# Reordering the output products of a fused attention and gated-FFN kernel: raw operands first, two pairs over two PSUM banks

## The chip, the core and the metric

The kernel runs on one core of a Trainium2 chip. The metric is the time of one execution on the device in microseconds (us). Before the change it is 850.09 us, the median of three runs (850.04 to 850.29). One more run was taken with the hardware profiler on: its span is 847.7 us, and all line numbers and profile times below come from it. The mean granted TensorE clock was 0.992 of full speed.

## What is computed

Two stages follow each other, over 4 batches of 6016 tokens with 256 channels:

```
qn = q / (norm of q over the tokens + 1e-6);  kn likewise
s  = kn^T @ qn / tau                          # 256 x 256 for each batch
a  = softmax(s)
x  = v @ a                                    # 6016 x 256 for each batch
gate = sigmoid(x @ w_gate);  val = x @ w_val  # 256 -> 1536
out  = (gate * val) @ w_out                   # 1536 -> 256, float32
```

The kernel never forms x. It multiplies the small softmax matrix into w_gate and w_val once for each batch (the tiles gh_G and gh_H), and so goes from v straight to gate and val.

## The kernel before

**Chunks and slots.** Tokens are worked on in chunks of 4 tiles of 128 tokens: 12 chunks for each batch (NCH), the last of them with 3 tiles. In a chunk the loop over f runs over 12 blocks of 128 hidden channels (FC = 12); one step of f is called a slot here. In a slot `glu` (line 460) issues two matmuls into ps_gate and two into ps_val (512 tokens wide), ScalarE takes the sigmoid of ps_gate into g_sb (line 481), and VectorE multiplies ps_val by it and writes one block of hT in bf16 (line 482). ps_gate and ps_val have two PSUM banks each.

**Output products.** The last product, hT with w_out, is done one chunk later, spread over the slots of the next chunk. It uses a scheme with seven products instead of eight for a 2 x 2 block product, in which the two token tiles of a pair p and tile p + 2 are one dimension, the two halves of the hidden channels the contraction, and the two halves of the 256 output channels the third. Of the seven products (PRODUCTS, line 33), n = 0 and 1 read hT itself; n = 2 to 6 read sums of hT blocks, which VectorE makes with `a_sum` (line 488, A_SUMS). Each product is 6 accumulating matmuls of 128 columns, so a chunk of 4 tiles has 2 pairs x 7 x 6 = 84 of them, called products in the rest of this text and counted from 0. The sums of the first half of the hidden channels (g = 0) are made in the chunk itself in slots 6 to 10, those of the second half (g = 1) in slots 0 to 4 of the next chunk.

**Banks and evictions.** Products 0 to 3 of a pair (n below FIRST_BANK) fill one PSUM bank of the pool pso, which has two, and products 4 to 6 another. When a bank is complete, `evict` (line 559) is put on the list `pending`; `flush()` (line 601), called after `glu` in each slot, issues it: a ScalarE copy into m_sb (line 564), and after a pair's second bank `combine` (line 515), five GpSimd operations (lines 522 to 528) that add the seven products up to out_sb. The last chunk of a batch has 3 tiles: one pair, and one tile whose product is done plainly (`single`, 12 matmuls of 256 columns). `store()` (line 606) writes out_sb to memory from SyncE's queue.

**The next batch beside it.** `side_work` (line 702) spreads the preparation of the next batch over the slots of the present one: loads of q and k, the score matmuls (ps_s, two of 256 columns about every second slot), squares on ScalarE (line 231), their accumulation on VectorE (line 269), and towards the end of the batch the folds of the accumulators (`acc_fold`, lines 279 to 287, six steps in consecutive slots from slot 2 of chunk 8), the norms (slot 9 of chunk 9), their root, their inversion (`wide_inv`, lines 309 and 310), scaling (line 320), exponentials (line 378), and the new gh tiles in chunk 11.

**Blocks.** The root and the exponentials need another activation table than the sigmoid. So at the end of chunks 9 and 10 a block stands after slot 11: half of the chunk's products (42) are held back and run there while ScalarE loads tables and works. In batch 3 there is no next batch, and so none of this.

The order on each engine is the order of the program: the kernel is recorded under a manual schedule. `run_work` (line 592) takes products from the list so that the remaining ones are spread evenly over the remaining slots, 7 to a slot in an ordinary chunk.

Of the kernel before, what the change touches and what calls it, by code (L numbers as in the profile page):

```python
# [16 lines left out]
A_SUMS = (  # L17
    ((0, 1), ALU.subtract, (1, 1)),
    ((0, 0), ALU.add, (1, 1)),
    ((0, 0), ALU.add, (0, 1)),  # L20
    ((1, 0), ALU.add, (1, 1)),
    ((1, 0), ALU.subtract, (0, 0)),
)
# [16 lines left out]
    (4, 4),  # L40
)
FIRST_BANK = 4


@with_exitstack
def kernel(
# [26 lines left out]
    B, N, C = q.shape  # L73
# [4 lines left out]
    FC = DFF // P  # L78
# [4 lines left out]
    NCH = (NT + TPC - 1) // TPC  # L83
# [446 lines left out]
    def out_work(b, ci):  # L530

        nt = groups[ci][1]
        half = nt // 2
        hT = hts[b, ci]
        work = []

        def product(state, p, n, i):
            a, w = PRODUCTS[n]
            bank, first = (0, 0) if n < FIRST_BANK else (1, FIRST_BANK)
            if n == first and i == 0:  # L540
                state[bank] = pso.tile([P, CH], FP32, tag="o", name="ps_o")
            g, j = divmod(i, FC // 4)
            if isinstance(a, tuple):
                lhsT = hT[:, 2 * i + a[1], ds((a[0] * half + p) * P, P)]
            else:
                lhsT = sums[b, ci, g][:, a, j, ds(p * P, P)]
            rhs = w_out_sb[:, 2 * i + w[0], ds(w[1] * P, P)] if isinstance(w, tuple) else w_sums[:, w, i, :]
            mm(
                state[bank][:, ds((n - first) * P, P)],
                lhsT,  # L550
                rhs,
                start=(n == first and i == 0),
                stop=(i == FC // 2 - 1),
                skip_group_check=True,
            )
            if i == FC // 2 - 1 and n in (FIRST_BANK - 1, len(PRODUCTS) - 1):
                pending.append((evict, state, bank, p))

        def evict(state, bank, p):
            if bank == 0:  # L560
                state["m"] = mpool.tile([P, len(PRODUCTS), P], FP32, tag="m", name="m_sb")
            n0, n1 = (0, FIRST_BANK) if bank == 0 else (FIRST_BANK, len(PRODUCTS))
            m = state["m"]
            nc.scalar.copy(m[:, n0:n1, :], state[bank][:, : (n1 - n0) * P].rearrange("p (n c) -> p n c", c=P))  # L564
            if bank == 1:
                combine(b, ci, p, m)
                if p == half - 1 and nt % 2 == 0:
                    stores.append((b, ci))

        def single(state, s, f):  # L570
            if f == 0:
                state["ps"] = pso.tile([P, CH], FP32, tag="o", name="ps_o")
            mm(state["ps"][:, :C], hT[:, f, ds(s * P, P)], w_out_sb[:, f, :], f == 0, f == FC - 1)
            if f == FC - 1:
                pending.append((evict_single, state, s))

        def evict_single(state, s):
            nc.scalar.copy(out_tile(b, ci)[:, s, :], state["ps"][:, :C])
            stores.append((b, ci))

        for p in range(half):
            state = {}
            for n in range(len(PRODUCTS)):
                for i in range(FC // 2):
                    work.append((1, product, state, p, n, i))
        if nt % 2:
            state = {}
            for f in range(FC):
                work.append((2, single, state, nt - 1, f))
        return work  # L590

    def run_work(work, share, keep=0):

        upto = sum(w[0] for w in work[: len(work) - keep]) * share
        done = 0
        while len(work) > keep and done < upto:
            cost, fn, *args = work.pop(0)
            fn(*args)
            done += cost

    def flush():
        while pending:
            fn, *args = pending.pop(0)
            fn(*args)

# [96 lines left out]
    def side_work(b):  # L702


        side = {}

        def at(slot, fn, *a):
            side.setdefault(divmod(slot, FC), []).append((fn, a))

        for ci in range(NCH):  # L710
            nb, nci = (b, ci + 1) if ci + 1 < NCH else (b + 1, 0)
            lb, lci = (b, ci + 2) if ci + 2 < NCH else (b + 1, ci + 2 - NCH)
            if (nb, nci) == (0, 1):
                at(8, lambda: transpose_v(0, 1, psm.tile([P, TPC * CB, P], BF16, tag="m", name="ps_tp")))
            elif nb < B:
                at(ci * FC + 2, transpose_v, nb, nci)
            if lb < B:
                at(ci * FC + 0, load_v, lb, lci)
            if (b, ci) == (0, 0):
                for i in range(FC // TPC):  # L720
                    at(i, load_w_out, i)
                    at(i + 2, sum_w_out, i)
        n = b + 1
        if n == B:
            return side
        first, last = (14 if b == 0 else 0), 8 * FC
        for g, (t0, nt) in enumerate(groups):
            s0 = first + g * (last - first) // NCH
            if b == 0:
                at(max(0, s0 - 12), load_qk, n, t0, nt)  # L730
            elif s0 >= 24:
                at(s0 - 24, load_qk, n, t0, nt)
            for u in range(nt):
                at(first + (t0 + u) * (last - first) // NT, score, n, t0, u)
            if g == 0:
                at(s0, acc_start, n)
            for i, (fn, w) in enumerate(((acc_square, 0), (acc_add, 0), (acc_square, 1), (acc_add, 1))):
                at(s0 + 1 + 2 * i, fn, n, g, w)
        if n + 1 < B:
            for g, (t0, nt) in enumerate(groups[:3]):  # L740
                at(NCH * FC - 24 + 8 * g, load_qk, n + 1, t0, nt)
        for i in range(6):
            at(8 * FC + 2 + i, acc_fold, n, *divmod(i, 3))
        at(9 * FC + 9, norms_mm, n)
        table = nc.scalar.preload_act_table
        for ci, s, *call in (
            (9, 0, wide_sqrt, n),
            (9, 0, table, ACT.Sigmoid),
            (9, 1, wide_inv, n, 0),
            (9, 2, wide_inv, n, 1),  # L750
            (10, 0, table, ACT.Exp),
            (10, 0, wide_scale, n),
            (10, 0, exps, n, 0),
            (10, 0, exps, n, 1),
            (10, 0, table, ACT.Sigmoid),
        ):
            side.setdefault((ci, FC + s), []).append((call[0], call[1:]))
        at(11 * FC + 0, sums_both, n)
        at(11 * FC + 0, gh_tiles, n)
        for i in range(len(gh_order)):  # L760
            at(11 * FC + min(i + 1, FC - 1), gh, n, i, *((pss, "s"), (psm, "m"))[i % 2])
        return side
# [6 lines left out]
    for b in range(B):  # L769
        side = side_work(b)  # L770
        for ci in range(NCH):
            block = b + 1 < B and ci in (9, 10)
            early = 1 if block else 2 if (b, ci) == (B - 1, NCH - 1) else 0
            for f in range(FC):
                first = (b, ci, f) == (0, 0, 0)
                glu(b, ci, f, (lambda: gh(0, 4, pso, "o", act=False)) if first else None)
                flush()
                if prev is not None:
                    if f == 4:
                        store()  # L780
                    if f < len(A_SUMS):
                        a_sum(*prev, 1, f)
                    held = len(work) if not block or f == 0 else held
                    run_work(work, 1 / max(1, FC - early - f), held // 2 if block else 0)
                if f >= FC // 2 and f - FC // 2 < len(A_SUMS) and (b, ci) != (B - 1, NCH - 1):
                    a_sum(b, ci, 0, f - FC // 2)
                for fn, a in side.get((ci, f), ()):
                    fn(*a)
                if (b, ci) == (0, 0):
                    for i in gh_first.get(f, ()):  # L790
                        gh(0, i, pso, "o")
            if prev is not None and block:
                flush()
                for s in range(3):
                    for fn, a in side.get((ci, FC + s), ()):
                        fn(*a)  # L796
                    run_work(work, 1 / (2 - s) if s < 2 else 1)
                flush()
            prev = (b, ci)
            if prev != (B - 1, NCH - 1):  # L800
                work = out_work(*prev)
# [40 lines left out]
```

## Time and profile before

| | us |
|---|---|
| median of the timed runs | 850.09 |
| span of the profiled run | 847.7 |
| head, until the first slot | 41.2 |
| batch 0, chunks 0 to 11 | 207.1 |
| batch 1 | 204.1 |
| batch 2 | 203.8 |
| batch 3, without the last chunk | 167.4 |
| last chunk and end | 24.1 |

The stages are read from the timeline, from the first ps_gate matmul of a chunk to that of a later one. Within a batch the chunks have different limits: chunks 0 to 8 carry the score matmuls and the squares of the next batch, chunks 9 and 10 end in blocks, chunk 11 makes the gh tiles, and batch 3 has the output work alone.

### The profile page before, as it was taken

Reading aid. Unit: us, or ns where it says so; the run is one execution under the profiler, and the core shown is the slowest. Engines: PE = TensorE matmul, PEld = TensorE weight load, DVE = VectorE, ACT = ScalarE, POOL = GpSimd, SP = SyncE. Lnnn points to the kernel's source line nnn. Section 1 sums busy time; section 2 is a strip of 40 time slices with the busy share of each in tenths; the row PEclk is TensorE's granted clock in tenths of the full one; section 3 lists DMA queues with packets and bytes.
Section 4 is the critical chain, followed back from the end, with each engine's and each line's share of the span. In section 5 each row is a group of like instructions: output and inputs, shape, how many; then the busy total and the mean of one; then the engine's idle time right before and its main releaser. Section 6 shows DMA issues by size and latency. Waiting matters only on the chain.

```text
span 847.7 us, 17813 instructions
## 1 busy us (share of the span) xinstructions
PE 798.8 (94%) x6760; PEld 499.0 (59%) x6772; DVE 741.2 (87%) x1236; ACT 531.7 (63%) x900; POOL 424.7 (50%) x623
## 2 busy tenths in 40 slices
PE   3799999999899999999989999999999999999996
PEld 2446666655566666665556666665565566666665
DVE  5688999999888999899978999999997988898884
ACT  3666667656766666665666667666576555555553
POOL 3564655443553656454544464645334355455543
PEclk9799999999999999999999999999999999999999
DMA  9976676432549556422275666622332422322401
GB/s 220 215 138 110 102 122 109 96 67 52 100 81 158 82 99 124 86 62 51 65 129 100 94 118 106 121 51 57 78 61 51 93 52 50 88 63 53 92 27 69
DMA packets 77926, 78.23 MB, mean 92 GB/s; under 512 B 50704, under 2 KB 55824, under 8 KB 77840
## 3 DMA queue, kind: packets, MB, share of 16 engines
q0 software_dynamic: 21216, 38.02, 27.2%
q1 hardware_dynamic: 56336, 38.48, 20.1%
q8 instruction: 53, 0.87, 0.4%
q10 hardware_dynamic: 288, 0.59, 0.2%
q14 instruction: 33, 0.27, 0.1%
HBM read 78.64 MB, written 24.64 MB: 122 GB/s over the span
## 4 chain that ended last, share of the span: by engine, by line
PE 73%; DVE 8%; ACT 7%; DMA 6%; issue 4%; POOL 2%; POOLq 0%; ACTq 0%; DVEq 0%
PE ps_gate L119 24%; PE ps_val L119 23%; PE ps_o L119 21%; DMA k_sb<-in_k_dram 6%; DVE sums L499 4%; DVE hT L482 4%; PE ps_s L119 3%; ACT g_sb L481 2%; PE ps_gh L119 2%; ACT sq L231 2%; ACT m_sb L564 1%; ACT L796 1%; POOL out_sb L525 0%; POOL m_sb L523 0%; DVE acc L269 0%
## 5 line engine op out<-in xcount | busy, mean ns | idle before, releaser
L481 ACT ACTIVATE g_sb<-ps_gate 128x512 f32<-128x512 f32 (+1 forms) x576 | 338.6, 588 | 273.0 <-PE ps_gate L119 259.1
L482 DVE TENSOR_TENSOR hT<-ps_val,g_sb 128x512 bf16<-128x512 f32 (+1 forms) x576 | 387.7, 674 | 78.1 <-ACT g_sb L481 71.0
L119 PE MATMUL ps_val<-vT,gh_H 128*128 128x512 bf16 (+1 forms) x1152 | 337.5, 374 | 3.7 <-DVE hT L482 3.4
L119 PE MATMUL ps_gate<-vT,gh_G 128*128 128x512 bf16 (+1 forms) x1152 | 337.5, 375 | 0.5
L499 DVE TENSOR_TENSOR sums<-hT 128x768 bf16<-128x768 bf16 (+1 forms) x470 | 305.2, 649 | 0.0
L522 POOL TENSOR_TENSOR m_sb<-m_sb 128x256 f32<-128x256 f32 x91 | 65.9, 724 | 383.4 <-ACT m_sb L564 383.4
L119 PEld LDWEIGHTS <-sums 128*128 128x128 bf16 x2730 | 187.9, 98 | 109.0 <-DVE sums L499 21.2
L119 PEld LDWEIGHTS <-gh_H 128*128 128x128 bf16 x1152 | 112.7, 98 | 136.8 <-issue 8.0
L119 PE MATMUL ps_o<-w_sums,sums 128*128 128x128 bf16 x1638 | 154.4, 219 | 1.9 <-DVE sums L499 1.7
L119 PE MATMUL ps_o<-w_out_sb,sums 128*128 128x128 bf16 x1092 | 109.9, 219 | 11.6 <-DVE sums L499 11.4
L119 PEld LDWEIGHTS <-hT 128*128 128x128 bf16 x1176 | 83.4, 98 | 55.3 <-issue 9.8
L525 POOL TENSOR_TENSOR out_sb<-m_sb 128x128 f32<-128x128 f32 x182 | 114.8, 650 | 0.0
L119 PEld LDWEIGHTS <-gh_G 128*128 128x128 bf16 x1152 | 96.8, 98 | 14.5 <-DVE gh_G L431 0.4
L119 PE MATMUL ps_o<-w_sums,hT 128*128 128x128 bf16 x1092 | 91.6, 219 | 8.6 <-ACT m_sb L564 8.3
L564 ACT COPY m_sb<-ps_o 128x512 f32<-128x512 f32 (+1 forms) x182 | 95.4, 528 | 0.1
L119 PE MATMUL ps_s<-k_sb,q_sb 128*128 128x256 bf16 x376 | 71.8, 295 | 17.9 <-DMA k_sb<-in_k_dram 10.6
L523 POOL TENSOR_TENSOR m_sb<-m_sb 128x256 f32<-128x256 f32 x91 | 81.1, 891 | 7.1
L528 POOL TENSOR_TENSOR out_sb<-m_sb 128x256 f32<-128x256 f32 x91 | 77.7, 853 | 0.0
L231 ACT ACTIVATE sq<-k_sb 128x1024 bf16<-128x1024 bf16 (+2 forms) x44 | 44.8, 1026 | 15.0 <-DMA k_sb<-in_k_dram 14.8
L269 DVE TENSOR_TENSOR acc<-acc,sq 128x1024 bf16<-128x1024 bf16 (+1 forms) x66 | 50.6, 766 | 0.0
L119 PEld LDWEIGHTS <-q_sb 128*128 128x128 bf16 x376 | 33.7, 105 | 23.5 <-issue 11.9
L231 ACT ACTIVATE sq<-q_sb 128x1024 bf16<-128x1024 bf16 (+2 forms) x36 | 36.5, 1015 | 0.2 <-DVE acc L659 0.2
(78 smaller groups left out, 276.6 us busy)
## 6 DMA issues: line engine op xcount, KB each, us to landing
out_dram<-out_sb SPq DMA_DIRECT2D x44, 512.0 KB, 3.4
v_sb<-in_v_dram POOLq DMA_DIRECT2D x44, 256.0 KB, 5.3
q_sb<-in_q_dram POOLq DMA_DIRECT2D x35, 256.0 KB, 6.9
k_sb<-in_k_dram POOLq DMA_DIRECT2D x35, 256.0 KB, 7.8
q_sb<-in_q_dram POOLq DMA_DIRECT2D x4, 512.0 KB, 12.7
k_sb<-in_k_dram POOLq DMA_DIRECT2D x4, 512.0 KB, 15.1
w_f<-in_moe_w_out_dram SPq DMA_DIRECT2D x3, 512.0 KB, 15.5
out_dram<-out_sb SPq DMA_DIRECT2D x3, 384.0 KB, 6.4
```

The source lines that it names most:

```text
L119: nc.tensor.matmul(out, lhsT=lhsT, rhs=rhs, start=start, stop=stop, **kw)
L231: nc.scalar.activation(out=sq[:, :nt, :], in_=src[:, :nt, :], func=ACT.Square)
L269: nc.vector.tensor_tensor(out=acc[:, :nt, :], in0=acc[:, :nt, :], in1=st[b]["sq", w][:, :nt, :], op=ALU.add)
L481: nc.scalar.activation(out=g_sb[:, :n], in_=ps_gate[:, :n], func=ACT.Sigmoid)
L482: nc.vector.tensor_tensor(out=hts[b, ci][:, f, :n], in0=ps_val[:, :n], in1=g_sb[:, :n], op=ALU.mult)
L499: nc.vector.tensor_tensor(out=sums[b, ci, g][:, m, :, : half * P], in0=hT[:, f0 + k0 : f1 : 2, ds(r0 * half * P, half * P)], in1=hT[:, f0 ...
L522: nc.gpsimd.tensor_tensor(out=t, in0=t, in1=m[:, 3:4, :].to_broadcast([P, 2, P]), op=ALU.add)
L523: nc.gpsimd.tensor_tensor(out=t, in0=t, in1=m[:, 4:6, :], op=ALU.subtract)
L525: nc.gpsimd.tensor_tensor(out=blocks[:, mids, :], in0=m[:, 1 - n, :], in1=m[:, 4 + n, :], op=ALU.add)
L528: nc.gpsimd.tensor_tensor(out=ends, in0=t, in1=m[:, 0:2, :], op=ALU.add)
L564: nc.scalar.copy(m[:, n0:n1, :], state[bank][:, : (n1 - n0) * P].rearrange("p (n c) -> p n c", c=P))
L796: fn(*a)
```

## The change

The order of the products, of what ScalarE and VectorE do for them, and of the batch ends is rearranged. No operation is added or removed: the counts of matmuls, copies and sums stay as they were.

- The products are issued in three rounds: n = 0 and 1 of both pairs, then n = 2 and 3 of both, then n = 4 to 6 of both. In each round pair 0 comes before pair 1, and each pair has one of the two banks. A chunk with an odd tile does that tile first.
- The g = 1 sums are made in slots 0, 1, 3, 4 and 5 (NEXT_SLOTS), the g = 0 sums in slots 7 to 11 (OWN_SLOTS).
- `flush(1)` issues one eviction for each slot; the store is issued at f = 6 instead of 4, and always asked for by the combine of the last pair.
- A block keeps 3/7 of the chunk's products (36) instead of 42, in one piece instead of three. In the two chunks that follow a block the products start at slot 2 (`late`).
- The two inversions of the norms move from the first block to slots 2 and 6 of chunk 10, and the folds are spread to every third slot.

It is meant to take products off operands that have only just been made, and to keep ScalarE's table loads and VectorE's folds from holding TensorE up.

```diff
+NEXT_SLOTS = (0, 1, 3, 4, 5)
+OWN_SLOTS = (7, 8, 9, 10, 11)
...
-                if p == half - 1 and nt % 2 == 0:
+                if p == half - 1:
                     stores.append((b, ci))
...
             nc.scalar.copy(out_tile(b, ci)[:, s, :], state["ps"][:, :C])
-            stores.append((b, ci))
-
-        for p in range(half):
-            state = {}
-            for n in range(len(PRODUCTS)):
-                for i in range(FC // 2):
-                    work.append((1, product, state, p, n, i))
+
+        states = [{} for _ in range(half)]
         if nt % 2:
             state = {}
             for f in range(FC):
                 work.append((2, single, state, nt - 1, f))
+        for n0, n1 in ((0, 2), (2, FIRST_BANK), (FIRST_BANK, len(PRODUCTS))):
+            for p in range(half):
+                for n in range(n0, n1):
+                    for i in range(FC // 2):
+                        work.append((1, product, states[p], p, n, i))
         return work
...
-    def flush():
-        while pending:
+    def flush(n=None):
+        for _ in range(len(pending) if n is None else min(n, len(pending))):
             fn, *args = pending.pop(0)
             fn(*args)
...
         for i in range(6):
-            at(8 * FC + 2 + i, acc_fold, n, *divmod(i, 3))
+            at(8 * FC + 1 + 3 * i, acc_fold, n, *divmod(i, 3))
...
-            (9, 1, wide_inv, n, 0),
-            (9, 2, wide_inv, n, 1),
...
+        at(10 * FC + 2, wide_inv, n, 0)
+        at(10 * FC + 6, wide_inv, n, 1)
...
             block = b + 1 < B and ci in (9, 10)
             early = 1 if block else 2 if (b, ci) == (B - 1, NCH - 1) else 0
+            late = 2 if b + 1 < B and ci in (10, 11) else 0
             for f in range(FC):
                 first = (b, ci, f) == (0, 0, 0)
                 glu(b, ci, f, (lambda: gh(0, 4, pso, "o", act=False)) if first else None)
-                flush()
+                flush(1)
                 if prev is not None:
-                    if f == 4:
+                    if f == 6:
                         store()
-                    if f < len(A_SUMS):
-                        a_sum(*prev, 1, f)
-                    held = len(work) if not block or f == 0 else held
-                    run_work(work, 1 / max(1, FC - early - f), held // 2 if block else 0)
-                if f >= FC // 2 and f - FC // 2 < len(A_SUMS) and (b, ci) != (B - 1, NCH - 1):
-                    a_sum(b, ci, 0, f - FC // 2)
+                    if f in NEXT_SLOTS:
+                        a_sum(*prev, 1, NEXT_SLOTS.index(f))
+                    if f >= late:
+                        keep = len(work) * 3 // 7 if block and f == late else keep if block else 0
+                        run_work(work, 1 / max(1, FC - early - f), keep)
+                if f in OWN_SLOTS and (b, ci) != (B - 1, NCH - 1):
+                    a_sum(b, ci, 0, OWN_SLOTS.index(f))
...
             if prev is not None and block:
-                flush()
-                for s in range(3):
-                    for fn, a in side.get((ci, FC + s), ()):
-                        fn(*a)
-                    run_work(work, 1 / (2 - s) if s < 2 else 1)
-                flush()
+                for fn, a in side.get((ci, FC), ()):
+                    fn(*a)
+                run_work(work, 1)
```

## The prediction

> **What bounds the kernel now.** First the page: which engine is busy, and which waits are counted against it.
>
> ```profile
> PE 798.8 (94%) x6760; PEld 499.0 (59%) x6772; DVE 741.2 (87%) x1236; ACT 531.7 (63%) x900; POOL 424.7 (50%) x623
> ...
> PE 73%; DVE 8%; ACT 7%; DMA 6%; issue 4%; POOL 2%; POOLq 0%; ACTq 0%; DVEq 0%
> ```
>
> TensorE carries the end; VectorE comes next. Then the table of waits: who holds TensorE up.
>
> ```profile
> PEld L119 <- DVE sums L499: 21.2, 41, 1.3
> PE ps_o L119 <- DVE sums L499: 13.1, 28, 1.1
> PE ps_o L119 <- ACT m_sb L564: 8.3, 6, 1.7
> PE ps_val L119 <- DVE hT L482: 3.4, 4, 0.9
> ```
>
> Products wait for sums of hT, and a few for an eviction. Matmul ends are modelled, so I measure a wait from start to start. The timeline of one chunk of batch 1 shows how:
>
> ```profile
> 336.47 0.33 PE L119 MATMUL ps_o<-w_out_sb,sums 128*128 128x128 bf16 x3
> 337.23 0.23 PE L119 MATMUL ps_o<-w_out_sb,sums 128*128 128x128 bf16 x1 [0.43 <-DVE sums L499]
> ```
>
> Three 128-wide matmuls take 3 x 0.0558 = 0.17 us, so the fourth was due at 336.64 and is 0.59 late. A slot (one f of a chunk) undisturbed is 4 x 0.2158 + 7 x 0.0558 = 1.254 us, 1.47 with a pair of score matmuls (both starts occur over and over). Adding up every late start over the timeline gives TensorE's true waits: **sums 24.9 us; evictions L564 9.3; hT L482 7.1; issue 2**. By chunk: chunks 1 to 7 of batches 1 and 2 lose 0.50 to 0.74 each to sums; chunks 1 to 10 of batch 3 only 0.13 to 0.48, mostly 0.26; batch 3's last 3.26; chunk 8 of batches 1 and 2 1.3 to sums plus 1.25 to hT; the chunks after the two blocks 1.18 and 1.91 to evictions. The windows of a middle chunk, a chunk of batch 3 and chunk 8:
>
> ```profile
> 331.46:348.57 17.11, 16.68 (x147) 10.56 (x144) 15.99 (x26) 11.56 (x19) 9.11 (x13) 1.00 0.58 110
> 716.09:731.42 15.33, 15.33 (x136) 9.40 (x133) 13.54 (x22) 8.87 (x16) 8.23 (x11) 1.00 0.31 69
> 382.57:400.19 17.62, 15.84 (x136) 9.38 (x133) 17.55 (x32) 8.86 (x16) 8.03 (x11) 1.00 0.32 61
> ```
>
> Columns: length, then PE, PEld, DVE, ACT, POOL busy. VectorE fills 15.99 of 17.11 in a middle chunk and all of chunk 8 (the folds), so it has about 1 us to give.
>
> **What the Trainium skill says.** "TensorE: Matmul & The Clock Gate", Back-to-back issue gap: N/2.4 + 2.5 ns between warm matmuls; the trace agrees (0.2158 and 0.0558 us). The same page, Architectural detail: ScalarE and VectorE are strict first-in first-out; here every copy indeed starts 0.50 us behind the sigmoid issued before it. "Perfetto Trace Analysis", Matmuls: groups should rotate through PSUM banks so that one is evacuated during the next; the kernel does, and the change alters the distance. "SBUF — State Buffer", SBUF: two separate sides: VectorE and GpSimd share an exclusive port pair; a 768-wide sum takes 0.54 us alone and 0.92 to 1.12 beside a combine.
>
> **Part 1, raw products first.** Per chunk 84 products run, 7 a slot. Now n = 0, 1 of both pairs come first (24 products, slots 0 to 3), so the late sums, issued in slots 0, 1, 3, 4, 5, are first needed at products 27, 33, 51, 57, 63, in slots 3, 4, 7, 8, 9. Each has at least three slots (4 us); the latest sum now ends about 3.3 us after its slot begins. **The 24.9 us of sums waits go.**
>
> **Part 2, the bank distance.** Both pairs hold both banks through n = 3. Pair 0's first bank is full at product 35 (slot 5), its copy is issued in slot 6 behind that slot's sigmoid, and product 48, the last of slot 6, needs that bank. The timeline gives the times from a slot's first matmul:
>
> ```profile
> 660.97 0.59 PE L119 MATMUL ps_gate<-vT,gh_G 128*128 128x512 bf16 x2
> 661.60 0.60 ACT L481 ACTIVATE g_sb<-ps_gate 128x512 f32<-128x512 f32 x1 [0.60 <-PE ps_gate L119]
> 662.10 0.58 ACT L564 COPY m_sb<-ps_o 128x512 f32<-128x512 f32 x1
> ```
>
> Sigmoid at +0.63, copy at +1.13, done at +1.71. In the blocks TensorE starts 0.06 after a copy's end (copy 416.96 to 417.54, matmul 417.60), so +1.77. TensorE is there at 0.863 + 6 x 0.0558 = 1.20. **New wait: 0.57 us in every chunk of 7 products a slot**: 8 + 8 + 8 + 10 = 34, or 19.4 us. Where the square of slot 5 (0.97 from its start to the next) precedes and that slot has no score, sigmoid 6 starts 0.22 later: 7 chunks, 1.5 us. Sum **20.9**. Behind the waiting product on TensorE stand the score pair and the next gate product, for which ScalarE, then VectorE wait; that gives VectorE 0.57 us to catch up. The other distances are harmless: pair 1's second bank is needed in slot 9 and copied in slot 7; across the chunk's end the copy of slot 0 ends at +1.60 and is needed in slot 1. Chunk 0, the chunks of 4 or 5 products a slot and the last chunk have a slot more between copy and need: nothing.
>
> **Part 3, blocks.** Before, 42 products run in a block and the next chunk's first product waits for two copies behind two table loads of 1.28 us. Now 36 run (2.01 us), the next two slots have no products, and the sigmoid goes first. First block, from slot 11's start: copy +1.13, load +1.65, root +2.94, load +3.35, sigmoid +4.64 to 5.24. TensorE has 0.86 + 2.01 + 2 x 0.86 = 4.60 of work, then needs that sigmoid's bank: 0.70, and 0.33 for hT behind it. So 1.03 for 1.43. Second block, the same with the exponentials: the row sums wait 0.4 for them, gate 0.6, hT 0.2, a gh bank 0.1: 1.3 for 1.91 plus small. Over three batches evictions and hT 10.0 become 7.0: **gain 3.0**.
>
> **Part 4, folds and inversions.** The same instructions, so no busy time is saved. Inversions (0.2 to 0.4 + 0.96 us each) move to slots 2 and 6 of chunk 10, which have no sum: hidden, as VectorE has 0.6 us free in such a slot and 1.2 us of lag before TensorE needs hT's bank. Folds go from consecutive slots to every third. The first (0.68 to 1.21) still meets a sum, in slots 1 and 10. My lag count (hT 0.60, sum 0.47 to 0.87, from start to next start) gives 0.4 to 2.1 us of hT waits a batch in chunks 8 and 9 against 1.25 to 1.5 before; I take 1.4: **no gain**.
>
> **Part 5, singles first, later store, the end.** Singles read hT only, their copy falls in slot 4: 0. The store at f = 6 waits for pair 1's combine, which ends near slot 5: hidden. In the last chunk pair 0's combine starts in slot 8 instead of 6, the pairs' combines queue (3.05 us each), and the last store goes out about 0.8 later: **cost 0.8**. With both combines end to end from slot 10 to slot 5, sums of slots 10 to 5 meet more contention. VectorE's hT then starts at most about 2.3 us into its slot, where TensorE would wait from 2.5: bound 0 to 5 us over 24 chunks, I take **1.5**.
>
> Sum: -24.9 + 20.9 - 3.0 + 0 + 0.8 + 1.5 = -4.7, from 850.1: **845.4 us, -0.55%**. Most of the gain is batch 3's last chunk and the blocks; batch 3's other chunks get slower by 0.3 each.
>
> **Rivals.** *VectorE becomes the bound*: hT lags over its bound in the busy chunks (+0.2 us more in 24 chunks, 4.8) and the folds take their upper end (+0.7 x 3 = 2.1): 852.3, **slower**. For it: 15.99 of 17.11; against: the 0.57 pause in slot 6 and empty slots 2 and 6. *The lag dissolves*: folds at 0.4 (-3.0), no contention (-1.5), blocks 0.4 better each (-2.4): 838.5. For it: in chunk 8 most hT lateness follows consecutive folds. *The eviction wait does not appear*, if slot 5's end runs early or the copy passes in time: 845.4 - 20.9 = 824.5. Against it: TensorE's order in the changed program puts product 48 in slot 6 with a wait on ScalarE. *A wash*: small errors leave 848.4 to 851.8.
>
> **Numbers.** My forecast 0.47 (843 to 848), lag dissolves 0.15, no eviction wait 0.06, wash 0.14, VectorE 0.18. Faster 0.68, same 0.14, slower 0.18. The range 838 to 853 leaves out the 824.5 and the far part of the VectorE case.
>
> **What would show it.** Waits of ps_o on sums near zero; waits of ps_o (w_out_sb, sums) on m_sb of some 0.5 us in 34 chunks, about 20 us in start-to-start time; chunks of batch 3 at 15.6 us instead of 15.33, its last chunk 3 us shorter; 17.0 us in middle chunks. I am wrong if batch 3's chunks get shorter (no eviction wait), or if ps_val waits on hT in middle chunks (VectorE).

## The result, and the profile after

The changed kernel takes **855.06 us** (median of 4 runs, 854.73 to 855.29); the kernel before, run beside it, 850.19 (850.04 to 850.73). The ratio is **1.0056 [1.0038, 1.0073]**: half a per cent slower, where 845.4 and a gain of half a per cent were forecast, and above the range's upper end of 853. The profiled span grew from 847.7 to 853.0 us.

First the page of the kernel after: TensorE's and VectorE's busy time, and the shares in the chain of waits.

```profile
PE 797.7 (94%) x6772; PEld 499.9 (59%) x6772; DVE 737.1 (86%) x1236; ACT 529.9 (62%) x900; POOL 427.8 (50%) x623
...
PE 71%; DVE 11%; ACT 7%; issue 6%; DMA 4%; POOL 0%; DVEq 0%; ACTq 0%; POOLq 0%
```

Busy times are those of before within 0.8%. The chain gives VectorE (DVE) 11% where it had 8%. The table of waits of the kernel after says which work it is (total, times, longest):

```profile
PE ps_o L121 <- ACT m_sb L566: 14.7, 34, 0.6
...
PE ps_val L121 <- DVE hT L484: 7.3, 17, 0.8
...
PE ps_gate L121 <- ACT g_sb L483: 3.3, 6, 0.6
```

No line of PE or PEld on the sums is left; before they were 21.2 + 13.1. In their place stands the eviction, exactly 34 times, and hT more than twice as long as before. Added up from start to start, as the prediction did:

| TensorE waits for | before, us | after, us |
|---|---|---|
| sums | 24.9 | 0 |
| evictions (m_sb) | 9.3 | 20.3 |
| hT | 7.1 | 17.2 |
| the sigmoid's bank (g_sb) | 0 | 4.3 |
| exponentials, gh tiles, row sums | 0.4 | 5.2 |
| together | 41.7 | 47.0 |

The prediction counted "issue 2" among TensorE's true waits. It is no wait. The trace before lacks twelve matmul records (PE x6760 beside PEld x6772; after the change both have 6772), ten of them of ps_gh, as here in chunk 11 of batch 1:

```profile
436.05 0.15 PEld L119 LDWEIGHTS <-e_sb 128*128 128x128 bf16 x2
436.11 0.38 PE L119 MATMUL ps_gh<-w_gate,e_sb 128*128 128x512 bf16 x1
436.54 0.49 PE L119 MATMUL ps_gate<-vT,gh_G 128*128 128x384 bf16 x2
```

Two weights are loaded and one matmul is shown, and the 0.43 us to the next start are two times 0.2158. Ten such gaps, three in each chunk 11 with a next batch and one in chunk 0, are not counted in the table.

So the waits have changed their owner and grown by 5.3 us. The last chunk's longer tail adds 0.8 and the head 0.2, and pieces below 0.04 us each are together 1.1 shorter: that makes the 5.2 us by which the span grew.

Where the waits are, by windows of the kernel after (length, then PE, PEld, DVE, ACT, POOL busy): a middle chunk and a chunk of batch 3, then chunks 9 and 10 of batch 1.

```profile
334.00:350.92 16.92, 16.52 (x147) 10.59 (x145) 15.49 (x26) 11.49 (x19) 9.47 (x14) 1.00 0.58 109
722.01:737.62 15.61, 15.21 (x136) 9.43 (x134) 14.00 (x23) 8.86 (x16) 7.49 (x12) 1.00 0.31 68
401.07:417.98 16.91, 15.85 (x141) 9.66 (x139) 16.23 (x29) 9.64 (x16) 7.44 (x10) 1.00 0.25 56
417.98:435.44 17.46, 15.98 (x135) 9.35 (x133) 14.92 (x27) 11.62 (x20) 9.75 (x15) 1.00 0.54 96
```

And chunks 9 and 10 of the kernel before, which the prediction did not show:

```profile
400.19:415.56 15.37, 15.37 (x142) 9.69 (x140) 13.75 (x25) 9.96 (x17) 5.82 (x9) 1.00 0.27 61
415.56:432.02 16.46, 15.43 (x136) 9.38 (x134) 15.55 (x28) 11.84 (x20) 9.21 (x17) 1.00 0.61 111
```

The middle chunk is 0.19 shorter and the chunk of batch 3 0.28 longer, as forecast. But chunk 9 grew by 1.54 and chunk 10 by 1.00, and there the forecast had nothing, or a gain. In batch 1 chunk 8 gained 1.08 (17.62 to 16.54), chunks 9 and 10 lost 2.54.

**The eviction wait, as forecast.** Timeline of slot 6 in a middle chunk of the kernel after:

```profile
325.27 0.59 PE L121 MATMUL ps_gate<-vT,gh_G 128*128 128x512 bf16 x2
...
325.90 0.60 ACT L483 ACTIVATE g_sb<-ps_gate 128x512 f32<-128x512 f32 x1
...
326.13 0.50 PE L121 MATMUL ps_o<-w_sums,sums 128*128 128x128 bf16 x6
...
326.39 0.58 ACT L566 COPY m_sb<-ps_o 128x512 f32<-128x512 f32 x1
...
327.02 0.22 PE L121 MATMUL ps_o<-w_out_sb,sums 128*128 128x128 bf16 x1 [0.40 <-ACT m_sb L566]
```

Sigmoid at +0.63, copy at +1.12, its end at +1.70; the seventh product, due at +1.20, starts at +1.75. The bracket says 0.40; from start to start it is 0.55.

**A fold in chunk 9.** Timeline of the kernel after:

```profile
401.32 1.21 DVE L281 TENSOR_TENSOR two<-acc 128x512 f32<-128x512 bf16 x1
...
402.45 0.68 DVE L484 TENSOR_TENSOR hT<-ps_val,g_sb 128x512 bf16<-128x512 f32 x1
...
403.05 0.62 DVE L501 TENSOR_TENSOR sums<-hT 128x768 bf16<-128x768 bf16 x1
403.18 0.59 PE L121 MATMUL ps_val<-vT,gh_H 128*128 128x512 bf16 x2 [0.37 <-DVE hT L484]
```

The slot began at 402.21, so ps_val was due at 402.64 and is 0.54 late: it needs the bank that hT reads until 403.13, and hT stood behind a fold of 1.21 us.

**An inversion in chunk 10.** Timeline of the kernel after:

```profile
423.60 0.29 DVE L311 TENSOR_SCALAR n_sb<-n_sb 128x130 f32<-128x130 f32 x1
...
423.93 0.97 DVE L312 RECIPROCAL n_sb<-n_sb 128x130 f32<-128x130 f32 x1
...
424.81 0.63 DVE L484 TENSOR_TENSOR hT<-ps_val,g_sb 128x512 bf16<-128x512 f32 x1
...
425.49 0.59 PE L121 MATMUL ps_val<-vT,gh_H 128*128 128x512 bf16 x2 [0.27 <-DVE hT L484]
```

The slot of that ps_val began at 424.63; it is 0.43 late. In chunk 10 five slots are late on hT in this way (0.30, 0.28, 0.43, 0.14, 0.53; together 1.68). Before, the same four instructions belonged to the block and ran while ScalarE loaded its table. The timeline of the kernel before shows VectorE with nothing else to do:

```profile
415.68 0.38 DVE L309 TENSOR_SCALAR n_sb<-n_sb 128x130 f32<-128x130 f32 x1 [1.34 <-ACT n_sb L304]
...
416.10 0.97 DVE L310 RECIPROCAL n_sb<-n_sb 128x130 f32<-128x130 f32 x1
...
416.98 0.18 DVE L309 TENSOR_SCALAR n_sb<-n_sb 128x128 f32<-128x128 f32 x1
417.19 0.95 DVE L310 RECIPROCAL n_sb<-n_sb 128x128 f32<-128x128 f32 x1
```

It idles 1.34 us before them, and its next hT starts at 418.46, behind a sigmoid that had to wait for the table load.

**The theory.** VectorE gains on TensorE only by the difference between a slot's length and its own work in it, hT and a sum, 0.60 + 0.47 = 1.07 us from start to start when undisturbed. By the number of products per slot, slots are 1.25 us long in chunk 8 (7 products), 1.09 to 1.14 in chunk 9 (4 or 5) and 1.14 to 1.20 in chunk 10 from slot 2 on (5 or 6). So a slot with a sum gives back 0.02 to 0.13 us in chunks 9 and 10, and two folds or two inversions there cannot be made good before TensorE wants a bank. The rivals: hT's lag comes from elsewhere (the order of the sums, contention with GpSimd), or the empty slots 0 and 1 after the blocks, or the eviction wait alone, make the loss.

### The profile page after: what moved, and what is told of

The parts are those of the page before. It is cut to its first block, busy times and chain, and to the rows that moved or that the text cites. A ratio compares the mean times of both kernels' runs of the same rounds, so it can differ in the third digit from the quotient of the medians.

```text
span 853.0 us, 17819 instructions
## 1 busy us (share of the span) xinstructions
PE 797.7 (94%) x6772; PEld 499.9 (59%) x6772; DVE 737.1 (86%) x1236; ACT 529.9 (62%) x900; POOL 427.8 (50%) x623
## 4 chain that ended last, share of the span: by engine, by line
PE 71%; DVE 11%; ACT 7%; issue 6%; DMA 4%; POOL 0%; DVEq 0%; ACTq 0%; POOLq 0%
PE ps_gate L121 24%; PE ps_val L121 22%; PE ps_o L121 20%; DVE hT L484 5%; DVE sums L501 3%; DMA k_sb<-in_k_dram 3%; PE ps_s L121 3%; ACT m_sb L566 3%; PE ps_gh L121 2%; ACT g_sb L483 2%; ACT sq L233 1%; DMA w_gate<-in_moe_w_gate_dram 1%; DVE acc L271 0%; ACT L306 0%; DVE gh_G L433 0%
## 5 line engine op out<-in xcount | busy, mean ns | idle before, releaser
L501 DVE TENSOR_TENSOR sums<-hT 128x768 bf16<-128x768 bf16 (+1 forms) x470 | 298.2, 634 | 0.0
L524 POOL TENSOR_TENSOR m_sb<-m_sb 128x256 f32<-128x256 f32 x91 | 75.1, 826 | 385.3 <-ACT m_sb L566 385.2
L121 PEld LDWEIGHTS <-sums 128*128 128x128 bf16 x2730 | 183.9, 98 | 80.9
L121 PE MATMUL ps_o<-w_sums,sums 128*128 128x128 bf16 x1638 | 144.0, 219 | 0.0
L121 PE MATMUL ps_o<-w_out_sb,sums 128*128 128x128 bf16 x1092 | 100.8, 219 | 14.7 <-ACT m_sb L566 14.7
L527 POOL TENSOR_TENSOR out_sb<-m_sb 128x128 f32<-128x128 f32 x182 | 110.0, 624 | 0.0
L566 ACT COPY m_sb<-ps_o 128x384 f32<-128x384 f32 (+1 forms) x182 | 96.2, 528 | 0.0
L525 POOL TENSOR_TENSOR m_sb<-m_sb 128x256 f32<-128x256 f32 x91 | 83.7, 919 | 7.1
L530 POOL TENSOR_TENSOR out_sb<-m_sb 128x256 f32<-128x256 f32 x91 | 74.8, 822 | 0.0
L271 DVE TENSOR_TENSOR acc<-acc,sq 128x1024 bf16<-128x1024 bf16 (+1 forms) x66 | 56.9, 863 | 0.0
```

The lines of the kernel that those rows point to most:

```text
L121: nc.tensor.matmul(out, lhsT=lhsT, rhs=rhs, start=start, stop=stop, **kw)
L271: nc.vector.tensor_tensor(out=acc[:, :nt, :], in0=acc[:, :nt, :], in1=st[b]["sq", w][:, :nt, :], op=ALU.add)
L501: nc.vector.tensor_tensor(out=sums[b, ci, g][:, m, :, : half * P], in0=hT[:, f0 + k0 : f1 : 2, ds(r0 * half * P, half * P)], in1=hT[:, f0 ...
L524: nc.gpsimd.tensor_tensor(out=t, in0=t, in1=m[:, 3:4, :].to_broadcast([P, 2, P]), op=ALU.add)
L525: nc.gpsimd.tensor_tensor(out=t, in0=t, in1=m[:, 4:6, :], op=ALU.subtract)
L527: nc.gpsimd.tensor_tensor(out=blocks[:, mids, :], in0=m[:, 1 - n, :], in1=m[:, 4 + n, :], op=ALU.add)
```

## The experiments

### Inversions back in the block

```diff
+            (9, 0, wide_inv, n, 0),
+            (9, 0, wide_inv, n, 1),
...
-        at(10 * FC + 2, wide_inv, n, 0)
-        at(10 * FC + 6, wide_inv, n, 1)
```

> The changed kernel with one part undone: the two inversions of the norms stand again in the first block, behind the root. Theory (VectorE lag): in chunk 10 of the changed kernel VectorE starts hT 2.0 to 3.1 us into every slot to slot 9, because the block leaves it 1.2 us late and 2.5 us of inversions are put on top while it has no reserve; taken out, chunk 10 falls from 17.46 to about 16.4 us and its hT waits from 1.69 to about 0.7; total 855.1 - 3 = 852. Rival (the two slots without products make the lag): chunk 10 stays over 17.0 us and the total within 1 us of the changed kernel.

Measured: **850.58 us** (850.33 to 851.16), ratio to before 1.0001 [0.9993, 1.001], 4.5 us less than the kernel after. Window of chunk 10 in this kernel:

```profile
416.65:433.02 16.37, 15.40 (x135) 9.37 (x133) 15.42 (x28) 11.62 (x20) 9.37 (x15) 1.00 0.53 96
```

17.46 became 16.37; its hT waits went from 1.68 to 0.54, while the sigmoid's bank still costs 0.77. Chunk 11 gained 0.27 more, as the exponentials are ready earlier. That is 1.36 a batch, 4.1 in all. The inversions made the loss in chunk 10.

### No empty slots after the blocks

```diff
-            late = 2 if b + 1 < B and ci in (10, 11) else 0
+            late = 0
...
                 run_work(work, 1)
+                flush()
```

The inversions stay in chunk 10.

> The changed kernel with the products of chunks 10 and 11 starting in slot 0 again and both evictions of the block issued at its end, so ahead of the next sigmoid; the inversions stay in chunk 10. Theory (VectorE lag): VectorE's work in chunk 10 is the same, so the wait only changes its name (to an eviction, some 1.2 to 1.9 us, as before the change) and chunk 10 stays at 17.2 us or more. Rival (empty slots): with products in slots 0 and 1 each slot is longer, hT is asked for less often, and chunk 10 falls to about 16.5 us, total 852.

Measured: **863.83 us** (863.59 to 865.69), ratio 1.0159 [1.0144, 1.0175]. In chunk 10 the theory held: hT waits of 1.37 remain, with 1.51 for evictions (17.90 in all). What I did not foresee is chunk 11: one wait of 2.98 us for an eviction behind the second block, and then a slower clock. Windows of this kernel, the stretch with the wait and the one behind it; the number after POOL's is PEclk:

```profile
436.00:443.00 7.00, 4.50 (x52) 3.26 (x51) 4.54 (x10) 5.35 (x8) 0.00 (x0) 1.00 1.10 182
443.00:447.00 4.00, 3.68 (x25) 2.35 (x25) 2.38 (x6) 1.55 (x5) 3.57 (x5) 0.58 0.04 9
```

25 matmuls take the 4 us. The edit undoes two things, the empty slots and the place of the block's evictions behind the next sigmoid. With the inversions in chunk 10 the two together are worth 8.8 us (863.83 less 855.06); no run takes them apart.

### Folds back in consecutive slots

```diff
-            at(8 * FC + 1 + 3 * i, acc_fold, n, *divmod(i, 3))
+            at(8 * FC + 2 + i, acc_fold, n, *divmod(i, 3))
```

> The changed kernel with the folds in six consecutive slots from slot 2 of chunk 8 again. Theory: spreading folds over slots that each have a sum makes VectorE late three times instead of once; undone, the hT waits of chunks 8 and 9 (0.94 + 1.56 us in batches 1 and 2) fall to about 1.3 together, total 855.1 - 3.5 = 851.5. Rival (the folds cost the same wherever they are, since VectorE has no reserve): 2.2 to 2.8 us together, total within 1 us of the changed kernel.

Measured: **850.23 us** (849.84 to 850.52), ratio 0.9996 [0.9987, 1.0005], 4.8 us less than the kernel after. Windows of chunks 8 and 9 in this kernel:

```profile
382.52:399.13 16.61, 15.74 (x137) 9.41 (x134) 16.54 (x32) 8.87 (x16) 8.94 (x11) 1.00 0.31 65
399.13:414.50 15.37, 15.37 (x142) 9.68 (x140) 14.29 (x26) 9.64 (x16) 7.33 (x10) 1.00 0.36 61
```

Chunk 9 is without a wait again. Chunk 8, with VectorE busy 16.54 of 16.61 us, waits 1.53 for hT but only 0.05 for the eviction: while TensorE waits for hT in slots 2 to 7, the copy of slot 6 is done meanwhile, so one wait covers the other. Spread, the two stand in a row. Together 3.06 in each of batches 1 and 2 became 1.58.

### The copy ahead of the next sigmoid

```diff
                         run_work(work, 1 / max(1, FC - early - f), keep)
+                        flush(1)
```

A bank that fills in a slot gets its copy in that slot, ahead of the next slot's sigmoid in ScalarE's queue.

> The changed kernel with one more flush(1) after the products of a slot, so that a full bank's copy is issued in the slot in which it is filled, ahead of the next slot's sigmoid. Theory (the eviction behind a sigmoid costs 0.56 us in each of 34 chunks): those waits go; chunks of batch 3 fall from 15.61 to about 15.1 us (-5.6 in all); middle chunks of batches 1 and 2 from 16.9 to 16.4 to 16.8, as VectorE loses the pause. Total 838 to 846. Rival (VectorE takes over, and the pause in slot 6 is what it needs): batch 3 falls, but middle chunks stay at 16.9 with waits on hT; total 848 to 850.

Measured: **834.36 us** (833.91 to 834.49), ratio 0.9807 [0.9793, 0.9822]: 20.7 us less than the kernel after, a little more than the theory's range. No wait of ps_o on m_sb is left; batch 3's chunks take 15.05 us for 15.61. Middle chunks keep 0.2 to 0.4 of hT waits that were not there with the eviction wait. So the gain is not those 34 waits alone: they are 20.2 us, hT's waits rose by 2.5, and waits after the blocks (2.0) and the end (0.9) fell.

### All three, and the two placements alone

The first of these kernels has the edits of the inversions, of the folds and of the copy; the second has the inversions and the folds as before the change and leaves the copy where the change has it. The latter is the kernel whose cost the prediction's sum describes, if folds and inversions cost nothing more than before.

> The changed kernel with three edits together: inversions back in the first block, folds back in consecutive slots, and a full bank's copy issued in the slot that fills it. If the three costs are separate, 855.1 - 4.5 - 4.9 - 20.7 = 825.0 us. Rival (VectorE is the bound once the eviction waits are gone, so that the savings overlap): 828 to 831.

> The changed kernel with the inversions back in the first block and the folds back in consecutive slots, the eviction behind the sigmoid left as it is. If the forecast failed by the placing of these two alone, this is the kernel that it described: 845.4 us, and by the two single runs 855.1 - 4.5 - 4.9 = 845.7. Rival (some of the cost lies elsewhere, in the order of products): 848 or more.

Measured: all three **826.75 us** (826.68 to 826.89), ratio **0.9723 [0.971, 0.9736]**, the fastest of all and 2.8% below the kernel before. The three single gains, 4.5 + 4.8 + 20.7, would give 825.0; 1.7 is missing, mostly because chunks 8 and 9 with the early copy lost 2.39 a batch to hT and gain only 1.03 from the folds' place. Page and windows (a middle chunk, a chunk of batch 3) of this kernel:

```profile
PE 791.9 (96%) x6772; PEld 498.9 (60%) x6772; DVE 720.1 (87%) x1236; ACT 538.4 (65%) x900; POOL 434.8 (53%) x623
```

```profile
340.33:356.88 16.55, 16.52 (x146) 10.56 (x144) 15.21 (x26) 11.60 (x20) 8.26 (x12) 1.00 0.30 66
773.99:789.04 15.05, 15.05 (x135) 9.39 (x133) 13.28 (x23) 9.10 (x16) 8.10 (x12) 1.00 0.28 63
```

TensorE is busy in all of a batch-3 chunk. In a middle one the profile has it busy 16.52 of 16.55 us, but with modelled ends; from start to start 0.20 us of hT waits are left there.

The two placements alone: **846.15 us** (845.73 to 846.32), ratio 0.995 [0.9938, 0.9962]. This is within 0.8 us of the forecast of 845.4. So the placing of folds and inversions is 8.9 of the 9.7 us by which the forecast missed. That the rest is so small is in part luck: chunks 10 and 11 of this kernel still wait 10.7 us where Part 3 put 7.0, and against that stand eviction waits of 19.2 for 20.9 (folds in consecutive slots cover the one of chunk 8) and 1.1 us less in chunk 0 and in pieces below 0.04 us.

### Folds every second slot, all in chunk 8

```diff
-            at(8 * FC + 1 + 3 * i, acc_fold, n, *divmod(i, 3))
+            at(8 * FC + 1 + 2 * i, acc_fold, n, *divmod(i, 3))
```

> The changed kernel with the folds in every second slot, 1 to 11 of chunk 8, instead of every third, which put the last two steps into chunk 9. Theory (reserve): VectorE gains on TensorE only where a slot is longer than its own hT and sum, some 1.07 us; slots of chunk 8 are 1.25, those of chunk 9 1.09 to 1.14. So folds cost little while they stay in chunk 8: waits of chunks 8 and 9 together 1.6 to 2.2 us a batch instead of 3.06, total 851.5 to 853. Rival (spreading itself costs, as each fold meets a sum and is waited for by itself): waits stay at 2.8 to 3.1, total 854.5 or more.

Measured: **851.5 us** (850.94 to 851.79), ratio 1.0013 [1.0006, 1.0019]. Windows of chunks 8 and 9 in this kernel:

```profile
383.51:400.05 16.54, 15.37 (x136) 9.42 (x134) 16.27 (x30) 8.87 (x16) 8.33 (x12) 1.00 0.40 65
400.05:415.80 15.75, 15.53 (x142) 9.66 (x140) 14.68 (x27) 9.64 (x16) 7.44 (x10) 1.00 0.35 60
```

Chunk 8 waits 1.50 as after the change, although it now holds six folds and not four; chunk 9 waits 0.39 for 1.56. That separates the two halves of the folds' loss: of the 1.48 a batch between spread and consecutive folds, 1.17 is that two of them fall into chunk 9's short slots, and 0.31 that they stand apart from the eviction wait. So spreading costs little where slots have room.

### The early copy in the kernel before

```diff
                     run_work(work, 1 / max(1, FC - early - f), held // 2 if block else 0)
+                    flush()
```

> The kernel before with the copy issued in the slot that fills the bank, as in the copy-first variant of the changed one. Theory (only the short distance between fill and reuse in the new order makes the copy's place matter): before, a bank is reused a whole group of 18 or 24 products later, so nothing is gained: within 1 us of 850.1. Rival (an earlier copy helps in either order, for instance by freeing GpSimd earlier): 847 or less.

Measured: **843.46 us** (842.21 to 844.67), ratio 0.9915 [0.9899, 0.993]. My expectation was wrong and the rival right: TensorE's waits for sums fell from 24.9 to 17.5 us, though none of them waits for a copy. The groups by line, the sums in the kernel before and then in this one (count, busy time, mean ns):

```profile
L499 DVE TENSOR_TENSOR sums<-hT 128x768 bf16<-128x768 bf16 (+1 forms) x470 | 305.2, 649 | 0.0
```

```profile
L499 DVE TENSOR_TENSOR sums<-hT 128x768 bf16<-128x768 bf16 (+1 forms) x470 | 278.8, 593 | 0.0
```

The same 470 sums take 56 ns less each; in a middle chunk 572 for 703 ns. GpSimd's combines start 0.9 to 1.5 us earlier in middle chunks, and fewer sums run beside them. The Trainium skill ("SBUF — State Buffer", SBUF: two separate sides) calls the port pair of VectorE and GpSimd an exclusive lock, which fits a sum of 0.54 us alone and of 0.90 to 1.12 where it starts after a combine's operation has; one that starts just ahead of such an operation takes 0.54. But I read this from the traces alone; no run moved the combines and nothing else. In the profiled execution a slower clock in two batches took 3.2 us of the gain back (see the last section).

### Each placement in the kernel before

The reverse test: the change's folds alone, and its inversions alone, in the kernel before.

```diff
-            at(8 * FC + 2 + i, acc_fold, n, *divmod(i, 3))
+            at(8 * FC + 1 + 3 * i, acc_fold, n, *divmod(i, 3))
```

> The kernel before with one part of the change alone: the folds in every third slot from slot 1 of chunk 8, two steps of them in chunk 9. Theory (chunk 9 has no reserve, wherever the products stand): chunk 9, which waits for nothing before, gets 1 to 1.6 us of waits on hT or sums a batch, chunk 8 gives back at most half of its 2.56, total 851 to 855. Rival (the folds cost more only with the new order of products): 850.4 or less.

```diff
-            (9, 1, wide_inv, n, 0),
-            (9, 2, wide_inv, n, 1),
...
+        at(10 * FC + 2, wide_inv, n, 0)
+        at(10 * FC + 6, wide_inv, n, 1)
```

> The kernel before with one part of the change alone: the inversions out of the first block, in slots 2 and 6 of chunk 10. Theory (VectorE is idle in the block and has no reserve in chunk 10): 2.5 us of VectorE work leave a place where it is free for one where it is late, chunk 10 grows by 0.7 to 1.5 us a batch, total 852 to 854.5. Rival (the 1.69 us came from the two slots without products that precede the inversions in the changed kernel): total within 0.8 us of 850.3.

Measured: folds **852.01 us** (851.2 to 853.73), ratio 1.0021 [1.0013, 1.003]. Windows of chunks 8 and 9 in the kernel with the folds spread:

```profile
385.70:402.31 16.61, 15.52 (x136) 9.38 (x133) 15.70 (x28) 8.86 (x16) 8.27 (x11) 1.00 0.29 65
402.31:418.98 16.67, 15.99 (x141) 9.63 (x139) 15.28 (x29) 9.96 (x17) 5.68 (x9) 1.00 0.25 57
```

In batches 1 and 2 chunk 8 loses 1.54 to waits for 2.54, chunk 9 1.32 for nothing: the same shape as in the changed kernel. In the profiled execution, one of the two slowest of 14, chunk 8 of batch 0 also met a slower clock.

Inversions **859.03 us** (858.14 to 859.38), ratio 1.0104 [1.0089, 1.0119], the direction of the theory but twice its upper end. Windows of chunk 10, and of the first two stretches of chunk 11, in the kernel with the inversions moved:

```profile
418.83:436.93 18.10, 15.81 (x135) 9.34 (x133) 15.14 (x28) 11.53 (x19) 9.22 (x15) 1.00 0.64 117
```

```profile
436.93:440.00 3.07, 0.91 (x9) 0.48 (x7) 0.09 (x1) 2.92 (x5) 1.60 (x4) 1.00 0.00 0
440.00:444.00 4.00, 3.78 (x27) 2.57 (x28) 2.77 (x6) 1.45 (x4) 3.60 (x6) 0.57 0.00 0
```

Chunk 10 is 1.64 longer (hT waits 1.87 for 0.25). The rest is in chunk 11: VectorE, late, scales the scores late, the exponentials and the copies behind them come late, TensorE's wait for the eviction grows from 1.91 to 2.33, and then, in two of the three batches, PEclk is 0.57 for 4 us.

## Why the prediction was wrong

**Right, by its own steps.** Part 1: the sums waits of 24.9 us are gone. Part 2: 34 eviction waits, 0.56 us each and 0.74 in 7 of them, together 20.3 against 20.9, with batch 3's chunks at 15.61 (forecast 15.6), middle chunks at 16.92 (17.0) and the copy at the very times forecast. Part 5: batch 3's last chunk lost its 3.26 us of waits and is with the end 2.4 shorter, so the end costs 0.8, as forecast. The contention lag, set at 1.5, measured 1.7, but that is luck: forecast for 24 chunks, it is in chunks 1 to 7 of batch 0 alone (hT waits 0.97 to 2.7), with none added in batches 1 and 2, and no run tells why. Two readings of the profile were wrong without harm to the sum: "issue 2" is missing records, and chunk 1 of batches 1 and 2 loses 0.32 to sums, not 0.50 or more.

**The step that failed, Part 4.** For the inversions I wrote "hidden, as VectorE has 0.6 us free in such a slot and 1.2 us of lag before TensorE needs hT's bank". One inversion is 0.3 + 0.97, which I took the 0.6 and the lag to swallow. But the lag was not free when it came: in chunk 10 VectorE is already behind, and what it loses it makes good by 0.13 us at most in each slot with a sum; the second inversion follows four slots later. The price was 1.36 us a batch in place of 0 (the experiment with the inversions back), and most of it fell into the first block of Part 3, whose "1.03 for 1.43" became 2.44: the sigmoid's bank at 0.77 as forecast (0.70), hT at 1.68 where 0.33 stood. With the inversions back, chunk 10 waits 1.30. In the second block, the "1.3 for 1.91" became 2.54, and 2.28 with the inversions back: the row sums waited 1.05 (0.78) for the exponentials and not 0.4, and what I put at 0.1 for a gh bank was 0.57 for gh tiles and row sums. So Part 3's "10.0 become 7.0" came out as 3 x (2.44 + 2.54) = 14.9. Of the 7.9 too much, 4.1 are the inversions and 3.8 are terms that were set too small: even with both placements undone, the blocks gained nothing on the kernel before (10.7 for 10.0).

For the folds I took 1.4 us of hT waits a batch, "no gain", from a range of 0.4 to 2.1. Measured is 2.50 in batches 1 and 2 (0.94 in chunk 8, 1.56 in chunk 9), above the upper end. The mechanism was the right one and its size was not: the count said nothing of the slots' lengths, and chunk 9's, with 4 or 5 products for 7, have no room for a fold (1.17 a batch by the experiment with all folds in chunk 8). Over three batches hT waits in chunks 8 and 9 came to 7.6 us for 4.0 before, where the sum had no change. What I also left out is that in chunk 8 the new eviction wait would have been covered by the folds, had they stayed together (0.05 for 0.56).

Blocks and folds are 11.5 us of error. Against them stand 0.6 us of eviction waits too many in the forecast and 1.4 us less in chunk 0 and in pieces below 0.04 us, which it did not name; the lag and the head add 0.4. That leaves the 9.9 us by which the span missed.

**The rivals.** "VectorE becomes the bound" gave 852.3 and named the folds' upper end; it was the nearest, though its other half, lag in all busy chunks, showed only in batch 0. It did not name the inversions. What would have shown it beforehand was in the profile: VectorE busy 15.55 of 16.46 us in chunk 10 of the kernel before, with the inversions' 2.5 us inside that sum, but at its very start, where the timeline has VectorE idle 1.34 us before them and a table load ahead of the next hT. Moving them out took them from time in which no hT could be made into time in which one was due every 1.14 to 1.20 us.

## What to carry to other kernels

Count the reserve of the second-busiest engine slot by slot, as the slot's length less that engine's own work in it: an operation that is moved costs its time over the reserve of the slots that follow, and one that stood in a block where the engine waited anyway was free there. Operations of about a slot's length belong into such blocks, or where slots are longest; even spreading over slots without reserve turns a short queue into a lasting lag. And when a bank is refilled soon after it is full, put its copy ahead of the next activation in the same queue: here one line took away 34 waits of 0.56 us that the reordering had brought, and with both placements undone the reordering's gain was there, 826.75 us for 850.37.

## What the runs showed of the hardware that I had not expected

A wait of TensorE can cost more than its length, because the granted clock falls to half after it. In all twelve traces the clock changes on a fixed grid: its whole stretches are multiples of 3.41 us (3.41, 6.83, 10.24, 13.65 and so on). I took all full-clock windows of this grid from 40 us to the last 8 us before the end, 2799 of them, and counted in each the time in which TensorE was late, from start to start. In eight windows this was 2.14 to 2.98 us, and after each of these eight, and after no other, one window followed at half clock, in which matmuls came 1.3 to 1.7 us late in sum. In all others it was 2.00 us or less. The eight are three in the kernel with no empty slots (the wait of 2.98 us in each batch), two in the early copy in the kernel before, two in the inversions moved there, and one in the folds spread there.

So the length of a wait does not decide alone. Windows of the early copy in the kernel before: a wait of 2.32 us inside one window and the window behind it, then a wait of the same 2.32 us in batch 2 that lies across two.

```profile
227.73:231.14 3.41, 1.25 (x16) 0.88 (x15) 0.36 (x1) 3.03 (x6) 0.83 (x2) 1.00 0.49 52
231.14:234.56 3.42, 3.42 (x20) 2.18 (x18) 2.61 (x7) 1.62 (x3) 3.34 (x6) 0.50 0.00 0
...
630.50:633.91 3.41, 2.29 (x34) 1.87 (x32) 1.56 (x4) 2.60 (x4) 2.28 (x4) 1.00 0.00 0
633.91:637.33 3.42, 2.38 (x27) 1.75 (x27) 1.62 (x3) 2.24 (x5) 1.89 (x3) 1.00 0.00 0
```

And in the kernel before with the folds spread, a wait of only 1.85 us with some 0.4 us of smaller ones in the same window:

```profile
182.94:186.35 3.41, 1.61 (x13) 0.59 (x11) 3.41 (x6) 0.60 (x1) 2.21 (x4) 1.00 0.27 92
186.35:189.76 3.41, 3.41 (x15) 1.73 (x16) 2.33 (x5) 1.07 (x2) 0.00 (x0) 0.50 0.75 141
```

After the waits of 1.91 us in the kernel before, chunk 11 shows 1.00 throughout. That the limit lies between 2.00 and 2.14 us of lateness in a window is an estimate from these traces; no run varied it on purpose.

The Trainium skill ("TensorE: Matmul & The Clock Gate", Part 1: The HAM clock gate) tells of a clock that halves after an idle window of about 3.4 us. The halving and the window's length agree; that the whole window has to be idle does not, since 2.14 of 3.41 us sufficed, and the measurement decides. It makes the empty slots and the late evictions after the blocks worth more than the waits that they remove: of the 10.9 us by which the profiled span grew without them (863.9 for 853.0; this was the slowest of the four runs), 4.6 are matmuls at that clock (1.67, 1.64 and 1.26 in the three batches).
